# x goes to DRAM once in float32: the sum of its two parts, written by GpSimd over the half batch's own output tile

## The chip, the core and the metric

The kernel runs on one NeuronCore of a Trainium2 chip. The metric is device time in microseconds (us) of one execution; lower is better. Three runs of the kernel before took 1088.52, 1089.51 and 1095.21 us (median 1089.51).

## What is computed

Attention over 4 batches, 8 heads, 576 positions and head size 64, in which only scores within tau of the row's maximum count, and then two gated layers over the 2304 tokens, each 512 to 2048 to 512:

```python
scores = scale * q @ k.T                       # per batch and head
scores = where(scores >= max(scores) - tau, scores, -1e9)
x  = softmax(scores) @ v                       # 2304 x 512 after joining heads
h  = x @ w_in;   x1 = (h * clip(h + 3, 0, 6) / 6) @ w_out
h2 = x1 @ w2_in; out = (h2 - tanh(h2)) @ w2_out
```

All inputs and the output are float32. The kernel holds a float32 operand of a matmul as two parts, a high part and what is left (a low part), and multiplies them in three passes.

## The kernel before, in words

**The work in order of time.** Attention goes by 144 units (128 queries of one head, or the last 64 of two heads) in the order of half batches (b, g): 4 batches, 2 halves each. The scores of a unit are one group of matmuls (line 678); VectorE and ScalarE make the maximum, the exponential and the threshold (lines 683 to 694); ScalarE writes the high part of the weights and GpSimd the low part (`pp`, line 705); SyncE issues a DMA that transposes `pp` into `pt` (line 708); PE multiplies by the values (line 731), four units later; ScalarE takes the result into the output tile `x` of the half batch (line 738; `xl` for the last 64 queries).

When a half batch is complete, `x_round` turns its output into the operand of layer 1, in two or three pieces (i = 0, 1 and, in the second half, i = 2 for `xl`): reciprocal of the sums (lines 763, 766), normalising multiply on GpSimd (line 778; for the very last piece i = 1 on VectorE), four PE transposes (line 773), the high part by ScalarE (line 784) and the low part by VectorE (line 786) into `xT`, which has 128 partitions, two parts, 4 column blocks and up to 320 tokens. `layer1` (lines 819 to 863) then multiplies with the first half of the hidden units (8 groups of 128, weights kept in SBUF), gates, multiplies with the second matrix and stores a first part of the result to `ys`. It is interleaved with the attention of the next half batch; the last `layer1`, of half batch (3, 1), stands alone at about 488 to 525 us.

**Why x goes to DRAM.** The second half of the hidden units has no room beside the attention. Its weights (`bw`, `bo`) come into memory that the attention's tiles give back, and its nine blocks of 256 tokens read x again from DRAM. Before, `layer1` stores both parts of `xT` (two DMAs for each half batch, lines 828 and 829) into `xs`, and `load_x` loads both (two DMAs a block, line 1038), finds the largest value by a row sum (line 456), and makes scaled float16 parts: ScalarE the high part (line 1043), VectorE in two steps the low part (lines 1045 and 1048).

**What sets the order.** Every piece of work is recorded as a task with an engine, a modelled duration, a key (its priority) and its buffers, and `Plan.issue` (line 103) plays the tasks through a model once, when the program is built: an engine that is free takes the ready task with the lowest key. So each engine, and the DMA queue of SyncE, has a fixed order in the program. A task is ready when the writers of the tiles it reads, and all users of the buffer's previous content, are done. Dependencies are kept for a whole buffer, not for its parts. A new tile of the second stage can be made only after all users of the attention's rings (`at_rings`, to which `x` and `xl` belong but `xT` does not; line 970) are done: this is the task `second_memory` (line 972). On the chip a tile that lies on memory of the attention waits for the last user of that memory.

Then comes layer 2, from about 711 us to the end, with weights prepared through DRAM.

Of the kernel before, what the change touches and what calls it, by code (L numbers as in the profile page):

```python
# [9 lines left out]
F32 = mybir.dt.float32  # L10
# [5 lines left out]
ACTF = mybir.ActivationFunctionType  # L16
ALU = mybir.AluOpType
# [183 lines left out]
def attention_moe_moe_kernel(  # L201
# [59 lines left out]
    XL, FO = 1, 7  # L261
# [18 lines left out]
    xs = dram.tile([128, 2, KD, NT], F32, name="xs")  # L280
    ys = dram.tile([128, KD, NT], F32, name="ys")
    NB = 256
# [464 lines left out]
    def x_round(b, g, i, key):  # L747
# [29 lines left out]
        def norm():  # L777
# [5 lines left out]
        add("pe", 0.00085 * KD * w, key, tr, r=[xt], w=[tp, xT])  # L783
        hi = add("act", t_act(KD * w), key + RK, lambda: nc.scalar.activation(
            out=xT.t[:, 0, :, cols], in_=pv(), func=ACTF.Copy), r=[tp], w=[xT])
        add("dve", t_dve(KD * w), key + RK, lambda: nc.vector.tensor_tensor(
            out=xT.t[:, 1, :, cols], in0=pv(), in1=xT.t[:, 0, :, cols].bitcast(F32), op=ALU.subtract),
            r=[tp], w=[xT], after=[hi])

# [29 lines left out]
    def layer1(b, g, W, key, width):  # L819
# [7 lines left out]
        x_stores[b, g] = [  # L827
            add("dma", 0.47, key + width * (1 + part) / 4, lambda part=part: nc.sync.dma_start(
                out=xs[:, part, :, c0:c0 + n], in_=xT.t[:, part, :, 0:n].bitcast(F32)), r=[xT], xfer=1.6)
            for part in range(2)]  # L830
# [34 lines left out]
    with tc.manual_schedule():  # L865
# [136 lines left out]
        R_xf = ring2([128, 2, KD, NB], F32, "xf", slot1=2)  # L1002
# [30 lines left out]
        def load_x(i, c, n, key):  # L1033
            xf, x = R_xf.new(), R_xh.new()
            after = writers(c, n)
            part = lambda i: xf.t[:, i, :, 0:n]
            for h in range(2):
                add("dma", 0.47, key - 16.0 + h, lambda h=h: nc.sync.dma_start(
                    out=part(h), in_=xs[:, h, :, c:c + n]), w=[xf], after=after, xfer=1.6)
            a = row_sums(lambda: part(0), xmax[:, i:i + 1], lambda: x.t[:, 0, :, 0:n], [xf], [x], key - 10.0, KD * n)  # L1040
            a = common(xmax[:, i:i + 1], top_x[i % 2], xpow[:, 0, i:i + 1], xpow[:, 1, i:i + 1], 2.0 ** -6, key - 9.0, [a])
            s = xpow[:, 1, i:i + 1]
            hi = add("act", t_act(KD * n, sbuf=True, scalars=True), key - 6.0, lambda: nc.scalar.activation(
                out=x.t[:, 0, :, 0:n], in_=part(0), func=ACTF.Copy, scale=s), r=[xf], w=[x], after=[a])
            lo = add("dve", t_dve(KD * n, scalars=True), key - 5.0, lambda: nc.vector.scalar_tensor_tensor(
                out=part(0), in0=part(0), scalar=s, in1=x.t[:, 0, :, 0:n],
                op0=ALU.mult, op1=ALU.subtract), r=[x], w=[xf], after=[hi])
            add("dve", t_dve(KD * n, scalars=True), key - 4.5, lambda: nc.vector.scalar_tensor_tensor(  # L1048
                out=x.t[:, 1, :, 0:n], in0=part(1), scalar=s, in1=part(0),
                op0=ALU.mult, op1=ALU.add), r=[xf], w=[x], after=[lo])  # L1050
            u = lambda k: unscale[:, k, i:i + 1]
            b = add("dve", 0.15, key - 3.5, lambda: nc.vector.tensor_scalar(
                out=u(0), in0=xpow[:, 0, i:i + 1], scalar1=wmax["bi"][:, 1:2], scalar2=GS,
                op0=ALU.mult, op1=ALU.mult), after=[a, scaled["bi"]])
            b2 = add("dve", 0.15, key - 2.5, lambda: nc.vector.tensor_scalar(
                out=u(1), in0=u(0), scalar1=wmax["bo"][:, 1:2], scalar2=1.0 / (6.0 * GS * GS * GS2),
                op0=ALU.mult, op1=ALU.mult), after=[b, scaled["bo"]])
            x_ready[i] = [b], [b2]
            return x
# [537 lines left out]
```

## Time and profile before

| what | value |
|---|---|
| median of three runs | 1089.51 us |
| the profiled execution | 1088.51 us, of which its span is 1086.7 us |
| PE busy | 1015.0 us (93%) |
| VectorE (DVE) busy | 847.6 us (78%) |
| ScalarE (ACT) busy | 718.6 us (66%) |
| GpSimd (POOL) busy | 339.0 us (31%), nearly all of it before 525 us |
| TensorE's granted clock, mean of the execution | 0.964 of full speed |

Busy time is summed over the instructions of an engine. A busy PE is not PE at its peak, since matmuls are pipelined and their ends are modelled. The stages differ, so the shares must be read by stretches of time.

### The profile page before, as it was taken

Reading aid. Unit: us, or ns where it says so; the run is one execution under the profiler, and the core shown is the slowest. Engines: PE = TensorE matmul, PEld = TensorE weight load, DVE = VectorE, ACT = ScalarE, POOL = GpSimd, SP = SyncE. Lnnn points to the kernel's source line nnn. Section 1 sums busy time; section 2 is a strip of 40 time slices with the busy share of each in tenths; the row PEclk is TensorE's granted clock in tenths of the full one; section 3 lists DMA queues with packets and bytes.
Section 4 is the critical chain, followed back from the end, with each engine's and each line's share of the span. In section 5 each row is a group of like instructions: output and inputs, shape, how many; then the busy total and the mean of one; then the engine's idle time right before and its main releaser. Section 6 shows DMA issues by size and latency. Waiting matters only on the chain.

```text
span 1086.7 us, 23294 instructions
## 1 busy us (share of the span) xinstructions
PE 1015.0 (93%) x8984; PEld 838.6 (77%) x8984; DVE 847.6 (78%) x1630; ACT 718.6 (66%) x1312; POOL 339.0 (31%) x353
## 2 busy tenths in 40 slices
PE   5668799999999899988999999999999999999998
PEld 4557788998999799978988888876676666666664
DVE  5889977687869788758797778889976796784564
ACT  6867979687967786645675566756755675574332
POOL 2656757666855675623000000000001111121000
PEclk8668899999999989998999999999999999999999
DMA  7899688967899989978657755432333866573335
GB/s 184 165 222 213 132 159 182 196 132 158 187 181 192 205 175 216 219 159 261 201 173 257 253 199 185 165 108 97 107 117 118 208 131 117 126 127 51 87 92 142
DMA packets 285007, 179.27 MB, mean 165 GB/s; under 512 B 202976, under 2 KB 257760, under 8 KB 284896
## 3 DMA queue, kind: packets, MB, share of 16 engines
q1 hardware_dynamic: 279088, 168.07, 61.0%
q0 software_dynamic: 5184, 9.44, 6.5%
q8 instruction: 71, 1.16, 0.5%
q14 instruction: 40, 0.33, 0.1%
q10 hardware_dynamic: 624, 0.26, 0.1%
HBM read 89.13 MB, written 46.14 MB: 124 GB/s over the span
## 4 chain that ended last, share of the span: by engine, by line
PE 58%; DVE 4%; ACT 1%; DMA 1%; issue 0%; SPq 0%; ACTq 0%; DVEq 0%
PE ya L489 24%; PE m L489 16%; PE h L489 10%; PE m L850 3%; PE s L678 2%; PE tp L731 1%; DMA y<-y 1%; PE h L850 1%; PE m L476 0%; DVE x L1276 0%; DMA st<-in_moe_w_in_dram 0%; DVE xh L1048 0%; DVE t L803 0%; PE tp L561 0%; DVE y L1175 0%
## 5 line engine op out<-in xcount | busy, mean ns | idle before, releaser
L705 POOL TENSOR_TENSOR pp<-e,pp 128x128 f16<-128x128 f32 (+3 forms) x156 | 181.1, 1182 | 120.3 <-issue 54.1
L489 PE MATMUL ya<-wo,g 128*128 128x512 f16 x864 | 205.4, 379 | 1.0 <-DVE g L813 0.6
L489 PEld LDWEIGHTS <-wi 128*128 128x128 f16 x1536 | 150.0, 98 | 40.4
L1416 POOL DMA_DIRECT2D po<-o x36 | 31.2, 876 | 459.7 <-ACT o L1410 459.7
L489 PEld LDWEIGHTS <-g 128*128 128x128 f16 x864 | 84.1, 98 | 79.3 <-DVE g L813 1.1
L683 DVE TENSOR_REDUCE z<-s 128x1 f32<-128x576 f32 x144 | 107.9, 753 | 45.4 <-PE s L678 44.7
L694 DVE SCALAR_TENSOR_TENSOR e<-s,z,e 128x576 f32<-128x576 f32 x144 | 115.8, 811 | 22.1 <-ACT e L685 17.1
L678 PE MATMUL s<-ks,q 128*128 128x288 f32 x512 | 105.9, 337 | 20.9 <-DVE e L694 20.1
L685 ACT ACTIVATE e<-s,z 128x576 f32<-128x576 f32 x144 | 105.0, 739 | 26.6 <-DVE z L683 20.3
L489 PE MATMUL m<-xT,ai 128*128 128x256 f32 (+1 forms) x720 | 112.8, 301 | 1.8 <-DVE st L426 0.6
L678 PEld LDWEIGHTS s<-ks,q 128*128 128x128 f32 x512 | 82.4, 212 | 29.4 <-DVE e L694 13.4
L489 PEld LDWEIGHTS m<-xT,ai 128*128 128x128 f32 x720 | 99.3, 190 | 3.7 <-DVE st L426 1.1
L489 PE MATMUL ya<-g,bo 128*128 128x256 f16 x864 | 101.1, 273 | 0.5 <-DVE g L813 0.5
L731 PE MATMUL tp<-vt,pt 128*128 128x65 f16 (+1 forms) x2240 | 88.4, 199 | 8.5 <-ACT q L591 2.4
L489 PE MATMUL m<-x,wi 128*128 128x256 f16 x768 | 95.2, 273 | 0.0
L731 PEld LDWEIGHTS <-pt 128*128 128x128 f16 (+1 forms) x2240 | 79.8, 104 | 16.7 <-DMA pt<-pp 6.0
L1381 ACT ACTIVATE t<-t,hid_s 128x512 f32<-128x512 f32 x72 | 51.6, 718 | 62.0 <-DVE t L1372 61.4
L489 PEld LDWEIGHTS <-bo 128*128 128x128 f16 x864 | 84.1, 98 | 10.6 <-issue 0.9
L489 PEld LDWEIGHTS <-bw 128*128 128x128 f16 x864 | 84.1, 98 | 10.4 <-issue 0.4
L813 DVE SCALAR_TENSOR_TENSOR g<-g,t 128x512 f16<-128x512 f16 x108 | 73.8, 686 | 20.7 <-ACT g L809 20.2
L809 ACT ACTIVATE g<-t 128x512 f16<-128x512 f32 x108 | 67.0, 624 | 33.7 <-DVE t L1383 26.0
L699 ACT ACTIVATE pp<-e 128x1152 f16<-128x1152 f32 (+1 forms) x80 | 85.1, 1064 | 5.0 <-DVE e L694 4.7
(177 smaller groups left out, 1878.0 us busy)
## 6 DMA issues: line engine op xcount, KB each, us to landing
st<-in_moe_w_in_dram SPq DMA_DIRECT2D x40, 512.0 KB, 5.0
st<-in_moe_w_out_dram SPq DMA_DIRECT2D x40, 512.0 KB, 4.4
xf<-xs SPq DMA_DIRECT2D x18, 512.0 KB, 5.2
y<-y SPq DMA_DIRECT2D x18, 512.0 KB, 3.8
po<-o POOLq DMA_DIRECT2D x36, 256.0 KB, 4.2
xs<-xT SPq DMA_DIRECT2D x8, 640.0 KB, 4.9
y<-ys SPq DMA_DIRECT2D x9, 512.0 KB, 5.9
po<-o SPq DMA_DIRECT2D x18, 256.0 KB, 2.0
```

The costliest lines, as they stand in the source:

```text
L489: nc.tensor.matmul(ps, l[a], r[b], start=first and t == 0 and i == 0, stop=last and t == 2 and i == n - 1,)
L678: nc.tensor.matmul(ps.t[:, half, 0:SH], l, ks[:, half * SH:(half + 1) * SH], start=i == 0, stop=i == len(ops) - 1,)
L683: add("dve", 0.69, key, lambda: nc.vector.tensor_reduce(out=z.t[:, 0:1], in_=s(), axis=AX.XY, op=ALU.max, negate=True), r=[ps], w=[z])
L685: exp = add("act", 0.66, key, lambda: nc.scalar.activation(out=ex(), in_=s(), func=ACTF.Exp, bias=z.t[:, 0:1]), r=[ps, z], w=[e])
L694: add("dve", 0.74, key, lambda: nc.vector.scalar_tensor_tensor(out=ex(), in0=s(), scalar=z.t[:, 1:2], in1=ex(), op0=ALU.is_ge, op1=ALU.mul ...
L699: high = add("act", t_act(w * S, sbuf=True), key, lambda: nc.scalar.activation(out=pp.t[:, 0:w, 0:S], in_=e.t[:, 0:w, :], func=ACTF.Copy), ...
L705: add(eng, dur, key, lambda src=src, dst=dst, queue=queue: queue.tensor_tensor(out=pp.t[:, 0:w, dst], in0=e.t[:, 0:w, src], in1=pp.t[:, 0: ...
L731: nc.tensor.matmul(pv.t[0:m, w_ * (D + 1):(w_ + 1) * (D + 1)], pt.t[:, n, blk, rows], vv, start=o == 0, stop=o == len(ops) - 1)
L809: hi = add("act", t_act(n, sbuf=True), key, lambda: nc.scalar.activation(out=gh(), in_=t(), func=ACTF.Copy, scale=GS2 if far else 1.0), r= ...
L813: go = lambda: nc.vector.scalar_tensor_tensor(out=gl(), in0=gh(), scalar=1.0 / GS2, in1=t(), op0=ALU.mult, op1=ALU.subtract)
L850: prev = [add("pe", t_mm(n, 1), kd, lambda p=p, l=l, r=r, m=m, s=s, ps=ps: nc.tensor.matmul(ps.t[:, 0:n], W["o", m].t[:, l, s], r[m].t[:, ...
L1381: add("act", t_act(2 * NB, sbuf=True, scalars=True), key, lambda: nc.scalar.activation(out=s_(), in_=h.t, func=ACTF.Tanh, scale=c), r=[h], ...
```

## The change

`xs` has room for one float32 array instead of two parts. After the high and the low part of a piece are in `xT`, GpSimd adds them (the transposed, normalised x) and writes the sum over the half batch's own output tile `x` (or `xl`), whose content has been transposed by then; a DMA stores it from there. Each piece is its own addition and its own DMA: 16 pieces of 128 tokens (512 elements a partition, runs of 512 bytes in DRAM) and 4 of 64 tokens (256 elements, runs of 256 bytes). The two stores of `layer1` fall away. `load_x` loads one array, and one VectorE step makes the low part.

```diff
-    xs = dram.tile([128, 2, KD, NT], F32, name="xs")
+    xs = dram.tile([128, KD, NT], F32, name="xs")
...
+    XL, FO, XWK = 1, 7, 12.0
...
-        add("pe", 0.00085 * KD * w, key, tr, r=[xt], w=[tp, xT])
+        turned = add("pe", 0.00085 * KD * w, key, tr, r=[xt], w=[tp, xT])
...
+        c0 = b * S + g * 256 + i * 128
+        xw = lambda: xt.t[:, c].rearrange("p h d -> p (h d)")[:, 0:KD * w].rearrange("p (k n) -> p k n", k=KD)
+        add("pool", t_pool(KD * w), key + XWK, lambda: nc.gpsimd.tensor_tensor(
+            out=xw(), in0=xT.t[:, 0, :, cols].bitcast(F32), in1=xT.t[:, 1, :, cols].bitcast(F32), op=ALU.add),
+            r=[xT], w=[xt], after=[lo, turned])
+        x_stores.setdefault((b, g), []).append(add("dma", 0.47, key + XWK + 2.0, lambda: nc.sync.dma_start(
+            out=xs[:, :, c0:c0 + w], in_=xw()), r=[xt], xfer=0.00625 * w))
...
-        x_stores[b, g] = [
-            add("dma", 0.47, key + width * (1 + part) / 4, lambda part=part: nc.sync.dma_start(
-                out=xs[:, part, :, c0:c0 + n], in_=xT.t[:, part, :, 0:n].bitcast(F32)), r=[xT], xfer=1.6)
-            for part in range(2)]
...
-        R_xf = ring2([128, 2, KD, NB], F32, "xf", slot1=2)
+        R_xf = ring2([128, KD, NB], F32, "xf", slot1=2)
...
-            for h in range(2):
-                add("dma", 0.47, key - 16.0 + h, lambda h=h: nc.sync.dma_start(
-                    out=part(h), in_=xs[:, h, :, c:c + n]), w=[xf], after=after, xfer=1.6)
+            add("dma", 0.47, key - 16.0, lambda: nc.sync.dma_start(
+                out=raw(), in_=xs[:, :, c:c + n]), w=[xf], after=after, xfer=1.6)
...
-            lo = add("dve", t_dve(KD * n, scalars=True), key - 5.0, lambda: nc.vector.scalar_tensor_tensor(
-                out=part(0), in0=part(0), scalar=s, in1=x.t[:, 0, :, 0:n],
-                op0=ALU.mult, op1=ALU.subtract), r=[x], w=[xf], after=[hi])
-            add("dve", t_dve(KD * n, scalars=True), key - 4.5, lambda: nc.vector.scalar_tensor_tensor(
-                out=x.t[:, 1, :, 0:n], in0=part(1), scalar=s, in1=part(0),
-                op0=ALU.mult, op1=ALU.add), r=[xf], w=[x], after=[lo])
+            add("dve", t_dve(KD * n, scalars=True), key - 5.0, lambda: nc.vector.scalar_tensor_tensor(
+                out=x.t[:, 1, :, 0:n], in0=raw(), scalar=s, in1=x.t[:, 0, :, 0:n],
+                op0=ALU.mult, op1=ALU.subtract), r=[xf], w=[x], after=[hi])
```

In the changed kernel the lines from 784 on stand a few lines lower or higher; the new addition is line 791, the new store line 794, the new load line 1040, and old lines 803, 1126 and 1128 are 810, 1125 and 1127.

**GpSimd, at the end of the first half batch** (`x` the output tile, `ao` and `ai` weights of layer 1, `pp` the attention weights). Before:

```order
L705 TENSOR_TENSOR pp<-e,pp 128x512
L778 TENSOR_TENSOR x<-x,rx 128x512
L451 TENSOR_TENSOR ao_1125<-st,ao_1125 128x512
L778 TENSOR_TENSOR x<-x,rx 128x512
L554 COPY qr<-qr 128x4x64
L705 TENSOR_TENSOR pp<-e,pp 128x2x64
L705 TENSOR_TENSOR pp<-e,pp 128x2x512
```

With the change:

```order
L705 TENSOR_TENSOR pp<-e,pp 128x512
L778 TENSOR_TENSOR x<-x,rx 128x512
L451 TENSOR_TENSOR ao_1125<-st,ao_1125 128x512
L554 COPY qr<-qr 128x4x64
L791 TENSOR_TENSOR x<-xT 128x512
L705 TENSOR_TENSOR pp<-e,pp 128x2x64
L451 TENSOR_TENSOR ai_1202<-st,ai_1202 128x512
L778 TENSOR_TENSOR x<-x,rx 128x512
```

The addition of the first piece stands ahead of a `pp`, and the normalising of the second piece has moved behind that addition, because both write the one buffer `x`.

**VectorE, at the end of the last half batch, about 482 to 490 us** (`rx`, `rl` reciprocals, `wu` and `st` weights of the second half, `tp` the bank of the transposes). Before:

```order
L763 SCALAR_TENSOR_TENSOR rx_7962<-x_7078,sv_5718 128x16
L766 RECIPROCAL rx_7962<-rx_7962 128x16
L778 TENSOR_TENSOR x_7078<-x_7078,rx_7962 128x512
L763 SCALAR_TENSOR_TENSOR rl_8006<-xl_7244,sv_5718 64x8
L766 RECIPROCAL rl_8006<-rl_8006 64x8
L786 TENSOR_TENSOR xT_8014<-tp_8000,xT_8014 128x4x128
L786 TENSOR_TENSOR xT_8014<-tp_8009,xT_8014 128x4x128
L418 TENSOR_SCALAR wu_8019<-wu_8019 128x512
L420 TENSOR_SCALAR wu_8019<-wu_8019 128x512
L786 TENSOR_TENSOR xT_8014<-tp_8022,xT_8014 128x4x64
```

With the change:

```order
L763 SCALAR_TENSOR_TENSOR rl_8020<-xl_7247,sv_5724 64x8
L766 RECIPROCAL rl_8020<-rl_8020 64x8
L786 TENSOR_TENSOR xT_8029<-tp_8023,xT_8029 128x4x128
L418 TENSOR_SCALAR wu_8038<-wu_8038 128x512
L778 TENSOR_TENSOR x_7083<-x_7083,rx_7980 128x512
L786 TENSOR_TENSOR xT_8029<-tp_8032,xT_8029 128x4x64
L420 TENSOR_SCALAR wu_8038<-wu_8038 128x512
L418 TENSOR_SCALAR wu_8044<-wu_8044 128x512
L423 SCALAR_TENSOR_TENSOR wu_8038<-st_7978,wu_8038 128x512
L786 TENSOR_TENSOR xT_8029<-tp_8047,xT_8029 128x4x128
```

The normalising of the second piece (line 778) has moved from ahead of the first low part (line 786) to behind it, and behind one step on weights; the second piece's low part, now the last of the three, stands behind three such steps.

**SyncE's DMA queue and ScalarE, at the change of memory, about 482 to 500 us** (`xs` in DRAM, `xf` the loaded x, a wait on DMAHW*n* is for an earlier DMA of that number). SyncE before:

```order
L406 DMA st_7960<-in_moe_w_in_dram 128x4x256 [waits DMAHW7_49]
L406 DMA st_7965<-in_moe_w_in_dram 128x4x256
L406 DMA st_7968<-in_moe_w_in_dram 128x4x256 [waits DMAHW1_49]
L828 DMA xs_60<-xT_8014 128x4x320 [waits Activation_49]
L1038 DMA xf_8055<-xs_60 128x4x256 [waits DMAHW3_49,DMAHW5_49,PE_49,Pool_49]
L1038 DMA xf_8055<-xs_60 128x4x256 [waits DMAHW4_49]
L1038 DMA xf_8068<-xs_60 128x4x256
L1038 DMA xf_8068<-xs_60 128x4x256 [waits DMAHW6_49]
L828 DMA xs_60<-xT_8014 128x4x320 [waits DMAHW7_49,DVE_49]
L406 DMA st_8102<-in_moe_w_in_dram 128x4x256 [waits DMAHW0_49,DVE_49]
```

With the change:

```order
L406 DMA st_7978<-in_moe_w_in_dram 128x4x256
L406 DMA st_7983<-in_moe_w_in_dram 128x4x256 [waits DMAHW3_49]
L406 DMA st_8017<-in_moe_w_in_dram 128x4x256
L794 DMA xs_60<-x_7083 512x1x128 [waits DMAHW5_49,Pool_49]
L794 DMA xs_60<-x_7083 512x1x128 [waits DMAHW6_49,Pool_49]
L794 DMA xs_60<-xl_7247 512x1x64 [waits DMAHW7_49,Pool_49]
L1040 DMA xf_8143<-xs_60 128x4x256 [waits DMAHW5_49,DMAHW6_49,DMAHW0_49,DMAHW7_49,PE_49,Activation_49]
L1040 DMA xf_8146<-xs_60 128x4x256 [waits DMAHW1_49]
L406 DMA st_8171<-in_moe_w_in_dram 128x4x256 [waits DMAHW2_49,DVE_49]
```

ScalarE with the change, over the same stretch:

```order
L807 ACTIVATE t_8082<-m_8058,three_131 128x320 [waits DMAHW7_49,PE_49,Activation_49]
L807 ACTIVATE t_8095<-m_8076,three_131 128x320 [waits DMAHW0_49,PE_49,Activation_49]
L816 ACTIVATE gh0_8103<-t_8082 128x320 [waits DVE_49]
L816 ACTIVATE gh2_8113<-t_8095 128x320 [waits DVE_49]
L1125 ACTIVATE bw_8141<-st_7978,wmax_122 128x512 [waits DMAHW6_49,DMAHW5_49,DMAHW7_49,Activation_49,Pool_49]
L1125 ACTIVATE bw_8152<-st_7983,wmax_122 128x512 [waits DVE_49]
L807 ACTIVATE t_8164<-m_8136,three_131 128x320 [waits DMAHW1_49,PE_49]
```

The three stores of the last half batch take the numbers 5, 6 and 7. With the change both the first load of `xf` and the first `bw` wait for these three; before, the stores read `xT` and neither waited for them.

## Rows read from the trace of the kernel before

**Rows 1.** The page's part 1: busy us, share of the span, instructions of each engine.

```profile
PE 1015.0 (93%) x8984; PEld 838.6 (77%) x8984; DVE 847.6 (78%) x1630; ACT 718.6 (66%) x1312; POOL 339.0 (31%) x353
```

**Rows 2.** Stretches of time: length, busy us of each engine, PEclk, DMA share, GB/s.

```profile
85.00:478.00 393.00, 368.67 (x4109) 348.04 (x4109) 309.89 (x588) 301.48 (x585) 249.60 (x252) 0.97 0.87 179
478.00:525.00 47.00, 39.62 (x308) 37.10 (x307) 36.00 (x83) 24.97 (x48) 12.66 (x10) 0.93 0.82 245
525.00:1071.00 546.00, 542.63 (x4134) 404.18 (x4133) 428.26 (x834) 327.79 (x559) 31.25 (x36) 1.00 0.52 145
```

**Rows 3.** Waits of PE, 85 to 478 us: total us, times, longest.

```profile
PE s L678 <- DVE e L694: 14.4, 14, 4.9
PE tp L731 <- DMA pt<-pp: 0.3, 1, 0.3
```

**Rows 4.** Groups on GpSimd by form: busy us, mean ns, idle before.

```profile
L816 POOL TENSOR_TENSOR gl<-t,gh 128x256 fp32r<-128x256 f32 x32 | 23.5, 738 | 15.7 <-ACT gh L809 15.3
L778 POOL TENSOR_TENSOR x<-x,rx 128x512 f32<-128x512 f32 x15 | 15.9, 1074 | 13.4 <-DVE rx L766 13.4
L451 POOL TENSOR_TENSOR ao<-st,ao 128x512 fp32r<-128x512 f32 x8 | 10.5, 1308 | 5.3 <-ACT ao L448 5.3
```

**Rows 5.** Instructions on the tile xf: min/median/max ns, first and last start us.

```profile
L1045 DVE SCALAR_TENSOR_TENSOR xf<-xf,xpow,xh x9: 1275/1278/1286, 503.5 to 678.1; 128x1024 f32<-128x1024 f32 x9
L1048 DVE SCALAR_TENSOR_TENSOR xh<-xf,xpow x9: 1268/1276/1767, 505.6 to 682.4; 128x1024 f16<-128x1024 f32 x9
```

**Rows 6.** Timeline, 482 to 491 us: start us, us, instruction, idle before and releaser.

```profile
483.21 0.69 DVE L778 TENSOR_TENSOR x<-x,rx 128x512 f32<-128x512 f32 x1
483.32 1.48 POOL L778 TENSOR_TENSOR x<-x,rx 128x512 f32<-128x512 f32 x1 [11.08 <-DVE rx L766]
...
484.86 1.09 PE L773 MATMUL tp<-ident,x 128*128 128x128 f32 x8
...
485.55 1.09 ACT L784 ACTIVATE xT<-tp 128x512 fp32r<-128x512 f32 x2 [0.40 <-PE tp L773]
...
486.80 0.69 ACT L414 ACTIVATE wu<-st 128x512 f32<-128x512 f32 x1 [0.16 <-DMA st<-in_moe_w_in_dram]
...
487.52 0.43 DVE L418 TENSOR_SCALAR wu<-wu 128x512 f32<-128x512 f32 x1
...
487.92 3.00 PE L489 MATMUL m<-xT,ai 128*128 128x320 f32 x12 [0.47 <-ACT xT L784]
...
488.32 0.42 DVE L786 TENSOR_TENSOR xT<-tp,xT 128x256 fp32r<-128x256 f32 x1
488.42 3.04 SPq L1038 DMA_DIRECT2D xf<-xs  x4
...
488.65 0.68 DVE L423 SCALAR_TENSOR_TENSOR wu<-st,wu 128x512 int32<-128x512 int32 x1
...
490.36 0.78 ACT L1126 ACTIVATE bw<-st,wmax 128x512 f16<-128x512 f32 x1 [1.26 <-DVE st L426]
```

**Rows 7.** The same view, 495 to 513 us.

```profile
495.78 1.05 ACT L456 ACTIVATE xh<-xf 128x1024 f16<-128x1024 f32 x1
...
511.83 0.47 ACT L809 ACTIVATE gh<-t 128x320 fp32r<-128x320 f32 x1 [3.94 <-DVE t L803]
...
511.85 0.85 PE L850 MATMUL h<-gh,ao 128*128 128x320 f32 x4 [2.82 <-DVE t L803]
```

**Rows 8.** A stretch after PE's idle at 480 to 488 us, columns as Rows 2.

```profile
490.00:492.00 2.00, 2.00 (x9) 2.00 (x8) 1.97 (x5) 1.64 (x3) 0.00 (x0) 0.50 0.92 186
```

**Rows 9.** DMA issues: instructions, KB each, median us from issue to landing.

```profile
xf<-xs SPq DMA_DIRECT2D x18, 512.0 KB, 5.2
xs<-xT SPq DMA_DIRECT2D x8, 640.0 KB, 4.9
wdo<-wu SPq DMA_DIRECT2D x16, 256.0 KB, 2.7
left<-in_k_dram SPq DMA_DIRECT2D x4, 128.0 KB, 4.7
```

More of the change, by code (lines that the diff above doesn't have):

```diff
@@ L260, in attention_moe_moe_kernel @@
     LK, LQ, LV, LD = 5, 3, 1, 4
-    XL, FO = 1, 7
+    XL, FO, XWK = 1, 7, 12.0
     XL3 = 40.0
@@ L782, in x_round @@
         add(*(("dve", t_dve(DM)) if tail else ("pool", t_pool(DM))), key - 7.0, norm, r=[xt, rx], w=[xt])
-        add("pe", 0.00085 * KD * w, key, tr, r=[xt], w=[tp, xT])
+        turned = add("pe", 0.00085 * KD * w, key, tr, r=[xt], w=[tp, xT])
         hi = add("act", t_act(KD * w), key + RK, lambda: nc.scalar.activation(
             out=xT.t[:, 0, :, cols], in_=pv(), func=ACTF.Copy), r=[tp], w=[xT])
-        add("dve", t_dve(KD * w), key + RK, lambda: nc.vector.tensor_tensor(
+        lo = add("dve", t_dve(KD * w), key + RK, lambda: nc.vector.tensor_tensor(
             out=xT.t[:, 1, :, cols], in0=pv(), in1=xT.t[:, 0, :, cols].bitcast(F32), op=ALU.subtract),
             r=[tp], w=[xT], after=[hi])
+        c0 = b * S + g * 256 + i * 128
[5 more added lines that the diff above has]
+            out=xs[:, :, c0:c0 + w], in_=xw()), r=[xt], xfer=0.00625 * w))
     def t_half(n, count):
@@ L1035, in load_x @@
             after = writers(c, n)
-            part = lambda i: xf.t[:, i, :, 0:n]
-            for h in range(2):
-                add("dma", 0.47, key - 16.0 + h, lambda h=h: nc.sync.dma_start(
-                    out=part(h), in_=xs[:, h, :, c:c + n]), w=[xf], after=after, xfer=1.6)
-            a = row_sums(lambda: part(0), xmax[:, i:i + 1], lambda: x.t[:, 0, :, 0:n], [xf], [x], key - 10.0, KD * n)
+            raw = lambda: xf.t[:, :, 0:n]
+            add("dma", 0.47, key - 16.0, lambda: nc.sync.dma_start(
+                out=raw(), in_=xs[:, :, c:c + n]), w=[xf], after=after, xfer=1.6)
+            a = row_sums(raw, xmax[:, i:i + 1], lambda: x.t[:, 0, :, 0:n], [xf], [x], key - 10.0, KD * n)
             a = common(xmax[:, i:i + 1], top_x[i % 2], xpow[:, 0, i:i + 1], xpow[:, 1, i:i + 1], 2.0 ** -6, key - 9.0, [a])
@@ L1043, in load_x @@
             hi = add("act", t_act(KD * n, sbuf=True, scalars=True), key - 6.0, lambda: nc.scalar.activation(
-                out=x.t[:, 0, :, 0:n], in_=part(0), func=ACTF.Copy, scale=s), r=[xf], w=[x], after=[a])
-            lo = add("dve", t_dve(KD * n, scalars=True), key - 5.0, lambda: nc.vector.scalar_tensor_tensor(
-                out=part(0), in0=part(0), scalar=s, in1=x.t[:, 0, :, 0:n],
-                op0=ALU.mult, op1=ALU.subtract), r=[x], w=[xf], after=[hi])
-            add("dve", t_dve(KD * n, scalars=True), key - 4.5, lambda: nc.vector.scalar_tensor_tensor(
-                out=x.t[:, 1, :, 0:n], in0=part(1), scalar=s, in1=part(0),
-                op0=ALU.mult, op1=ALU.add), r=[xf], w=[x], after=[lo])
+                out=x.t[:, 0, :, 0:n], in_=raw(), func=ACTF.Copy, scale=s), r=[xf], w=[x], after=[a])
+            add("dve", t_dve(KD * n, scalars=True), key - 5.0, lambda: nc.vector.scalar_tensor_tensor(
+                out=x.t[:, 1, :, 0:n], in0=raw(), scalar=s, in1=x.t[:, 0, :, 0:n],
+                op0=ALU.mult, op1=ALU.subtract), r=[xf], w=[x], after=[hi])
             u = lambda k: unscale[:, k, i:i + 1]
```

## Prediction

> **What bounds the kernel now.** I read the shares of the span first: PE is busy 93% of it, VectorE 78%, GpSimd 31% [rows 1]. These are means over unlike stages, so the table by stretches came next [rows 2]. From 525 to 1071 us PE is busy 542.6 of 546.0 us: whatever another engine saves there is hidden, up to 3.4 us. In the attention, 85 to 478 us, PE is busy 368.7 of 393.0 us and leaves 24.3 us; GpSimd is busy 249.6 us (64%). The waits show what PE stood still for: 14.4 us for VectorE's thresholded scores, but only 0.3 us for the transposed weights that come from GpSimd by way of a DMA [rows 3]. So GpSimd has slack there. In 478 to 525 us, where the attention ends and its memory changes hands, PE leaves 7.4 us. The timeline of that stretch is the one to read closely [rows 6, 7], since the change touches it in two places.
>
> **The change, part by part.**
>
> *Layer 1's second half, 525 us on.* Nine VectorE steps fall away, each with a median of 1.28 us [rows 5], together 11.5 us, and nine of eighteen loads of 512 KB [rows 9]. PE covers all of this [rows 2]: I take nothing, with a gain of at most 3.4 us. Were the cover gone, the 11.5 us would count.
>
> *Attention: the additions.* Before the last half batch there are 14 additions of 512 elements and 3 of 256. The trace has no such addition; nearest are GpSimd's normalising multiply of the same size, 1.07 us, and its subtraction of two float32 tiles of that size, 1.31 us; for 256 elements 0.74 us [rows 4]. With 1.19 between the two, 14 x 1.19 + 3 x 0.74 = 18.9 us. GpSimd goes from 249.6 to about 268 us of 393 (68%). I take nothing on the path, because PE hardly waits for what GpSimd makes [rows 3]; the cover is GpSimd's idle and the four units that the weighting lags behind. Without the cover it is all 18.9 us. Below nothing the bound is the 14.4 us that PE waits for VectorE: another order could shorten them, and nothing excludes it.
>
> *Attention: the second piece behind the first.* The planner holds dependencies for the whole buffer, so the second piece's normalising now waits until the first piece has been turned, split and added. PE's work at these places is otherwise the scores of the next half batch, which are ready; I take nothing, except at the end, where no next half batch follows.
>
> *The stores.* Two of up to 640 KB for each half batch become two or three of 256 or 128 KB, 20 for 16, with half the bytes. The DMA engines are busy 87% of the attention [rows 2], but PE does not wait for them; nothing.
>
> *The end of the attention.* Here the price is. First, the last piece's normalising on VectorE stood at 483.21 us [rows 6]. Now it stands behind the step of line 418, which ended at 487.95 because ScalarE's step before it had waited for a weight DMA until 486.80 [rows 6]. Then come 0.69 for the normalising, half of 1.09 for its four transposes, half of 1.09 for the high part [rows 6]: 489.7 instead of the 487.92 at which PE began, so 1.8 us late. Its low part now stands behind the other piece's (0.42) and three weight steps (0.43, about 0.43 and 0.68): from 488.64 to 490.6, and 0.69 more gives 491.3. Before, the last low part ended at 488.74. Second, the tiles of the next stage wait for the three stores, as the order shows. The addition of the piece (1.19) and of the short one (0.74) end at 493.2; for a store the nearest row is a 256 KB store from SBUF, 2.7 us to landing [rows 9], which makes 495.9. ScalarE's first `bw`, before at 490.36, comes 5.5 us later. The loads of x go out at 495.9 instead of 488.42, and with 5.2 us to landing [rows 9] the row sum of line 456 starts at 501.1 instead of 495.78: 5.3 us late. Between it and the last gate (511.83 us) VectorE did four steps of 1.28 us; two remain, which gives 2.6 back [rows 5]. The gate, and with it PE's second product at 511.85 [rows 7], come 5.3 - 2.6 = 2.7 us late, and nothing behind it is idle enough to win them back [rows 2].
>
> A bound above for the last store: it writes runs of 256 bytes, and the only rows with such runs, 128 KB loads of k, take 4.7 us [rows 9], 2.0 us more. The Trainium skill speaks against this piece: "DMA: Bandwidth & Descriptors", Specifications, asks for at least 512 bytes a transfer for full rate and says that below this the engine reads, modifies and writes. By that rule the term would be 4.7 us instead of 2.7; no store with such runs is in the trace, so it does not decide. I stay with the store row, since half the bytes go. If ScalarE, not VectorE, carries the gate, the 2.6 us don't come back: 5.3. PE also ran at half clock (0.50, 1.2 GHz) in 490 to 492 us after its idle [rows 8]; a longer idle can add about 1 us of that. Ends: 2.7 + 2.0 + 2.6 + 1.0 = 8.3 us above; below, the stretch's whole idle gone, -7.4 us.
>
> *Sum.* The rows are of an execution of 1088.51 us (span 1086.7 and 1.8 around it). 0 + 0 + 2.7 gives 1091.2. The median of the runs is 1.0 above that execution, so 1092.2 us on the scale of the median.
>
> **The rivals.**
>
> *The transition costs nothing.* PE has eight groups of matmuls of the last layer 1 in front of it, and six can run before a bank must come back; ScalarE's 3.94 us and PE's 2.82 us of idle before the gate [rows 7] may swallow the delay. Then the median stays at 1089.5. Against it: those idles are VectorE's backlog, and the loads now start 7 us later. Chance 0.20.
>
> *Faster.* VectorE's backlog bounds 478 to 525 us (it is busy 36.0 of 47.0 [rows 2]), and it loses two of four large steps there, while the DMAs move half the bytes. If the stores land early enough that only this counts, the idle of the stretch goes: 1089.5 - 7.4 = 1082.1, and with the 3.4 us behind it 1078.7. It decides if the row sum starts before about 498 us. Chance 0.13.
>
> *Slower: GpSimd's queue.* GpSimd runs in order. An addition waits for VectorE's low part, and the weights' low part (`pp`) behind it waits too, then the transposing DMA, then PE. Of the 17 additions before the last half batch, 10 stand right ahead of a `pp`, two of them short: 8 x 1.19 + 2 x 0.74 = 11.0 us, so 1103; with all 17 it is 18.9, so 1111. It decides once the delay is longer than the lag of four units covers. For it: GpSimd is idle in pieces, not as a block. Against it: the 0.3 us [rows 3]. Chance 0.18.
>
> *Slower: both engines at one port.* GpSimd's multiply that ran beside VectorE's at 483.2 took 1.48 us [rows 6], where the mean is 1.07 [rows 4]: 0.41 longer. If each of 20 additions loses or costs that once on the path, 8.2 us: about 1100. Against it: most of VectorE's work in the attention takes one input from PSUM. Chance 0.07. The Trainium skill ("SBUF — State Buffer", Who interferes with whom) has the rule: a GpSimd instruction that reads SBUF and a VectorE instruction with two SBUF inputs share a port, and the later one is blocked entirely. The longer row agrees in kind, at 0.41 us.
>
> **How the numbers follow.** The forecast has 0.42, the rivals 0.20, 0.13, 0.18 and 0.07. The time is the forecast's, 1092.2; its own range is about 1088 to 1098. The range from 1082 to 1106 takes in the stretch's idle gone on one side, and additions that stand ahead of a `pp` on the other; what is left out is the far half of the faster case and of GpSimd's queue. One per cent, about what a measurement of this kernel can tell from no change, is 10.9 us: below 1078.6 or above 1100.4. Faster: the faster case's far end and some luck in the attention's order, 0.08. Slower: three quarters of GpSimd's queue, half of the port and the forecast's upper tail, 0.18. The same: 0.74.
>
> **What would show it.** Right: the first `bw` and the row sum near 496 and 501 us with a DMA as what they waited for; PE's gap before its second product still there and some 2.7 us later; from there to the end the same length as before; 85 to 478 us within 3 us. Wrong: PE waiting for `pt` by several us in the attention (GpSimd's queue); `pp` or VectorE steps longer where an addition runs (the port); the row sum at or before 498 us, or a span of 525 to 1071 us that shrinks by more than 3.4 us, which would say that PE's busy time there hides a wait.

## The result, and the profile after

The kernel before has a median of 1089.28 us over 15 runs, the changed one 1097.14 us (1092.32 to 1100.37, 15 runs): a ratio of 1.0062, 95% interval [1.0047, 1.0077]. That is slower by 0.6%, inside the one per cent that I called the same, and 4.9 us above the forecast of 1092.2. The profiled execution of the changed kernel took 1094.55 us (span 1092.8), 6.1 us longer in span than the one of before, and is itself 2.6 us below the median of its runs.

The page's part 1 of the changed kernel answers to [rows 1]:

```profile
PE 1016.1 (93%) x8984; PEld 841.0 (77%) x8984; DVE 839.5 (77%) x1621; ACT 718.8 (66%) x1312; POOL 362.6 (33%) x373
```

GpSimd has 20 instructions and 23.6 us more, VectorE nine instructions and 8.1 us less. The three stretches of [rows 2] again (length, busy us of each engine in the order PE, weight load, VectorE, ScalarE, GpSimd, then the granted clock, DMA share, GB/s):

```profile
85.00:478.00 393.00, 365.37 (x4082) 345.74 (x4081) 307.17 (x587) 300.74 (x583) 268.70 (x269) 0.97 0.83 169
478.00:525.00 47.00, 38.44 (x295) 35.84 (x295) 34.43 (x76) 22.88 (x45) 16.62 (x13) 0.89 0.57 162
525.00:1071.00 546.00, 543.63 (x4143) 406.73 (x4143) 423.60 (x830) 330.50 (x563) 31.32 (x36) 1.00 0.51 142
```

PE is as full as before from 525 us on. The waits of PE between 85 and 478 us, for [rows 3]:

```profile
PE s L678 <- DVE e L694: 15.9, 14, 2.6
...
PE tp L731 <- DMA pt<-pp: 0.7, 2, 0.4
```

So GpSimd's 19 us more still do not reach PE by way of the transposed weights. Most of the time went into the end of the attention, as a_last_dma below shows. Here is its timeline in the changed kernel (start us, us, instruction, idle before and what ended it), to be read beside [rows 6]:

```profile
485.25 1.04 POOL L778 TENSOR_TENSOR x<-x,rx 128x512 f32<-128x512 f32 x1 [12.77 <-DVE wmax L1112]
...
488.50 1.26 POOL L791 TENSOR_TENSOR x<-xT 128x512 f32<-128x512 f32 x1 [0.73 <-DVE xT L786]
...
488.86 1.20 DVE L418 TENSOR_SCALAR wu<-wu 128x512 f32<-128x512 f32 x1 [0.49 <-ACT wu L414]
...
489.97 0.68 DVE L778 TENSOR_TENSOR x<-x,rx 128x512 f32<-128x512 f32 x1
...
490.80 0.63 PE L773 MATMUL tp<-ident,x 128*128 128x128 f32 x4 [2.51 <-DVE x L778]
...
492.11 6.89 PE L489 MATMUL m<-xT,ai 128*128 128x320 f32 x36 [0.69 <-ACT xT L784]
...
492.94 1.66 POOL L791 TENSOR_TENSOR x<-xT 128x512 f32<-128x512 f32 x1 [3.17 <-DVE xT L786]
493.38 1.51 DVE L420 TENSOR_SCALAR wu<-wu 128x512 int32<-128x512 int32 x1
...
494.57 0.92 POOL L791 TENSOR_TENSOR xl<-xT 128x256 f32<-128x256 f32 x1
494.81 0.96 DVE L418 TENSOR_SCALAR wu<-wu 128x512 f32<-128x512 f32 x1
495.51 0.51 SPq L794 DMA_DIRECT2D xs<-xl  x1
...
497.80 1.54 SPq L1040 DMA_DIRECT2D xf<-xs  x2
...
498.79 1.39 ACT L1125 ACTIVATE bw<-st,wmax 128x512 f16<-128x512 f32 x2
```

The new order can be followed line by line: the first piece's multiply (485.25), its addition (488.50), only then the second piece's multiply on VectorE (489.97), PE's first product of layer 1 at 492.11 instead of 487.92, the last addition, the last store (495.51), and when it has landed the loads of x (497.80 instead of 488.42) and the first `bw` (498.79 instead of 490.36). The waits of SyncE's queue show that the loads did stand for that store (us, times, longest):

```profile
SPq L1040 <- DMA xs<-xl: 0.6, 1, 0.6
```

The timeline further on, for [rows 7], with the gate's product (516.22 us, 511.85 before) and the first product of the second half of the hidden units (530.11 us, 524.48 before):

```profile
502.76 1.04 ACT L456 ACTIVATE xh<-xf 128x1024 f16<-128x1024 f32 x1
...
516.22 1.44 PE L853 MATMUL h<-gh,ao 128*128 128x320 f32 x4 [2.59 <-DVE t L810]
...
530.11 2.79 PE L489 MATMUL m<-xh,bw 128*128 128x256 f16 x24
```

From there to the end it is 562.7 us, before 1086.7 - 524.48 = 562.2. The DMA issues that answer to [rows 9] (KB each, median us to landing):

```profile
xf<-xs SPq DMA_DIRECT2D x9, 512.0 KB, 4.4
xs<-x SPq DMA_DIRECT2D x16, 256.0 KB, 3.0
...
xs<-xl SPq DMA_DIRECT2D x4, 128.0 KB, 2.3
```

### The profile page after: what moved, and what is told of

Read it like the earlier page. It is cut to its first block, busy times and chain, and to the rows that moved or that the text cites. A ratio compares the mean times of both kernels' runs of the same rounds, so it can differ in the third digit from the quotient of the medians.

```text
span 1092.8 us, 23307 instructions
## 1 busy us (share of the span) xinstructions
PE 1016.1 (93%) x8984; PEld 841.0 (77%) x8984; DVE 839.5 (77%) x1621; ACT 718.8 (66%) x1312; POOL 362.6 (33%) x373
## 4 chain that ended last, share of the span: by engine, by line
PE 83%; DVE 7%; ACT 4%; DMA 3%; issue 2%; SPq 1%; POOL 0%; DVEq 0%; ACTq 0%; POOLq 0%
PE ya L489 25%; PE m L489 22%; PE h L489 11%; PE m L853 8%; PE s L678 7%; PE tp L731 6%; DVE e L694 2%; PE tp L561 2%; DMA pt<-pp 1%; DVE z L683 1%; DVE ks L586 1%; ACT ks L584 1%; PE h L853 1%; ACT e L685 1%; PE m L476 1%
## 5 line engine op out<-in xcount | busy, mean ns | idle before, releaser
L694 DVE SCALAR_TENSOR_TENSOR e<-s,z,e 128x576 f32<-128x576 f32 x144 | 116.2, 812 | 12.6 <-ACT e L685 6.4
L678 PEld LDWEIGHTS s<-ks,q 128*128 128x128 f32 x512 | 83.4, 215 | 36.1 <-DVE e L694 22.7
L489 PEld LDWEIGHTS m<-xT,ai 128*128 128x128 f32 x720 | 102.2, 195 | 3.6 <-DVE t L810 1.5
```

The source lines that it names most:

```text
L489: nc.tensor.matmul(ps, l[a], r[b], start=first and t == 0 and i == 0, stop=last and t == 2 and i == n - 1,)
L678: nc.tensor.matmul(ps.t[:, half, 0:SH], l, ks[:, half * SH:(half + 1) * SH], start=i == 0, stop=i == len(ops) - 1,)
L694: add("dve", 0.74, key, lambda: nc.vector.scalar_tensor_tensor(out=ex(), in0=s(), scalar=z.t[:, 1:2], in1=ex(), op0=ALU.is_ge, op1=ALU.mul ...
```

## A mark to count from

All executions come to the end of the attention at different times, so I count from one event: the start of GpSimd's last multiply of line 778 on `x`, called the mark. It lies at 483.32 us before and at 485.25 in the changed kernel. In the changed kernel and in the experiments below that edit its last half batch alone, the instructions stand in the same order up to there; the kernel before has another order. Four columns are us behind the mark, from the timelines, the fourth of them the end of the span. PE idle and PE busy are what lies between the mark and the first product `xh,bw`; the last column is the ratio to the kernel before.

| kernel | mark | first `bw` | row sum, line 456 | first product `xh,bw` | end | PE idle | PE busy | ratio, 95% |
|---|---|---|---|---|---|---|---|---|
| before | 483.32 | 7.0 | 12.5 | 41.2 | 603.4 | 5.2 | 35.9 | 1 |
| changed | 485.25 | 13.5 | 17.5 | 44.9 | 607.6 | 8.0 | 36.9 | 1.0062 [1.0047, 1.0077] |
| after_again | 488.91 | 14.3 | 18.3 | 44.4 | 606.0 | 7.3 | 37.1 | 1.0046 [1.0028, 1.0064] |
| a_last_dma | 483.66 | 6.8 | 11.2 | 39.1 | 601.1 | 5.2 | 33.9 | 0.9986 [0.9968, 1.0004] |
| b_last_order | 487.01 | 10.6 | 14.8 | 43.1 | 606.1 | 6.6 | 36.6 | 1.0047 [1.0029, 1.0066] |
| b_last_again | 489.81 | 10.7 | 14.8 | 43.3 | 605.7 | 6.6 | 36.7 | 1.0042 [1.0026, 1.0059] |
| f_serial | 489.12 | 11.4 | 16.0 | 42.8 | 604.6 | 6.7 | 36.1 | 1.0018 [1.0003, 1.0032] |
| f_serial_again | 489.93 | 11.4 | 15.9 | 40.1 | 602.1 | 6.0 | 34.1 | 1.0014 [0.9998, 1.0030] |
| h_adds_only | 485.99 | 8.8 | 11.9 | 42.9 | 604.8 | 6.7 | 36.2 | 1.0041 [1.0022, 1.0059] |

Between the first product `xh,bw` and the end every one of them needs 561.6 to 563.0 us. So the price stands ahead of that product: in the 41 us behind the mark, and in when the mark comes.

Even behind the mark one execution is not like another of the same program. f_serial and f_serial_again differ by 2.7 us at the first product, 2.0 of it in PE's busy time, for the same matmuls. The stretch from 24 to 28 us behind the mark shows what differs (columns as [rows 2]; f_serial first):

```profile
513.12:517.12 4.00, 4.00 (x18) 3.98 (x18) 3.24 (x8) 3.34 (x7) 2.89 (x2) 0.57 0.21 51
513.93:517.93 4.00, 3.49 (x24) 3.22 (x22) 3.70 (x7) 2.83 (x5) 2.37 (x3) 1.00 0.80 249
```

The granted clock was 0.57 in one, mostly the half level of 1.2 GHz, and full (2.4 GHz) in the other. So two microseconds of busy time between two lines of the table can be the clock's and need not be the edit's.

## The experiments

**The whole end of the attention undone: a_last_dma.** Theory: the price is made in the last half batch. Rival: GpSimd's queue in the attention. The last half batch has no addition; the transposed tile is stored as before, with the low part accumulated onto the high one by a DMA.

```diff
+        if (b, g) != (B - 1, 1):
             add("pool", ...)  # the addition and its store
...
+        if (b, g) == (B - 1, 1):
+            x_stores[b, g] = [add("dma", ..., lambda: nc.sync.dma_start(
+                out=xs[:, :, c0:c0 + n], in_=xT.t[:, 0, :, 0:n].bitcast(F32)), ...)]
+            x_stores[b, g].append(add("pool", ..., lambda: nc.gpsimd.dma_start(
+                out=xs[:, :, c0:c0 + n], in_=xT.t[:, 1, :, 0:n].bitcast(F32), accum_op=ALU.add), ...))
```

> The changed kernel, but the last half batch alone sends x to DRAM from the operand tile xT, its high part by a store and its low part by an accumulating DMA from GpSimd; there is no addition and no store from the output tile at the end of the attention. Theory 1 (the price is made at the end of the attention, by the second piece that waits for the first and by the next stage's tiles that wait for three late stores): the first bw goes back from 498.8 to about 491 us, the row sum from 502.8 to about 497 us, PE's second product comes 4 to 6 us earlier, and the time falls from 1097.1 to about 1092 us. Theory 2 (GpSimd's additions delay the attention before that): at most 1 us comes back, about 1096 us. Theory 3 (VectorE is the bound at the gate, whatever the loads do): the row sum comes earlier but the second product stays near 516 us, about 1096 us.

Measured: 1088.97 us, ratio 0.9986 [0.9968, 1.0004]. The timeline of the end of the attention:

```profile
487.85 2.03 PE L489 MATMUL m<-xT,ai 128*128 128x320 f32 x12 [0.50 <-ACT xT L784]
...
488.54 1.89 SPq L1047 DMA_DIRECT2D xf<-xs  x2
...
490.45 0.76 ACT L1132 ACTIVATE bw<-st,wmax 128x512 f16<-128x512 f32 x1
...
494.82 1.06 ACT L456 ACTIVATE xh<-xf 128x1024 f16<-128x1024 f32 x1 [0.84 <-DMA xf<-xs]
```

Product, loads and `bw` stand where they stood in [rows 6], although the other 17 additions still run. Undoing the last half batch alone takes the whole price away, and the time is 3 us below the 1092 that I expected. The run undoes additions, order and stores together.

**The order of its pieces undone: b_last_order, b_last_again.** The second piece's multiply no longer stands behind the first one's addition. The additions, the stores and the wait for them stay.

```diff
+        end = (b, g) == (B - 1, 1)
...
-            r=[xT], w=[xt], after=[lo, turned])
+            r=[xT, xt] if end else [xT], w=[] if end else [xt], after=[lo, turned])
...   # the store now names the addition as what it waits for
```

> The changed kernel, with one dependency less in the planner for the last half batch: the second piece's normalising no longer waits for the first piece's addition, while the three stores from the output tile stay, and with them the wait of the next stage's tiles. Theory 1: the first product of the last layer 1 starts about 2.5 us earlier (489.6 instead of 492.1 us), the stores land about 2 us earlier, and the time falls by 1.5 to 2.5 us to about 1095 us; the difference to the kernel without the stores is what the wait for memory costs, about 3 us. If the order of the pieces is the whole price, it falls by 5 to about 1092 us; if it is none of it, it stays at 1097.

> b_last_order once more: if the order is worth as much beside the stores as it was without them (f_serial against a_last_dma, 3.9 us), 4 us below the change of this call; if the wait for the stores hides most of it, 1 to 2 us below.

Measured: 1096.14 us (1.0047) and 1094.99 us (1.0042), the latter 1.3 us below the changed kernel that ran beside it (after_again). Of the first, the products and what the next stage waits for:

```profile
491.22 6.51 PE L489 MATMUL m<-xT,ai 128*128 128x320 f32 x32 [0.52 <-ACT xT L784]
...
496.15 1.25 SPq L1041 DMA_DIRECT2D xf<-xs  x2
...
497.62 0.74 ACT L1126 ACTIVATE bw<-st,wmax 128x512 f16<-128x512 f32 x1
```

The first product is back to 4.2 us behind the mark (6.9 in the changed kernel), yet nearly all of the price is left: beside the stores, the order is worth 1 us or so by the medians, which these runs can't tell from nothing.

**The additions elsewhere: d_double_add.** Every addition of the first seven half batches runs twice.

```diff
-        add("pool", ..., lambda: nc.gpsimd.tensor_tensor(...)
+        add("pool", ..., lambda: [nc.gpsimd.tensor_tensor(...)
+            for _ in range(1 if (b, g) == (B - 1, 1) else 2)],
```

> The changed kernel in the same order, with every addition of the first seven half batches done twice on GpSimd (17 more instructions, about 20 us of GpSimd time). Theory 1 (the additions in the attention are hidden): no more than 1.5 us, about 1098 us, and PE's waits for the transposed weights stay under 2 us in 85 to 478 us. Theory 2 (GpSimd's queue carries the additions to the path): 10 to 19 us more, 1107 to 1116 us, PE waiting for pt or VectorE's scores later by that. A port shared with VectorE: VectorE's steps of the attention get longer where an addition runs, 3 to 8 us more, about 1102 us.

Measured: 1098.43 us, 1.0068 [1.0050, 1.0086]; the changed kernel's interval holds it. Stretch and wait, 85 to 478 us (two views):

```profile
85.00:478.00 393.00, 366.65 (x4046) 346.68 (x4044) 304.88 (x584) 300.67 (x582) 287.91 (x285) 0.95 0.81 167
```

```profile
PE tp L731 <- DMA pt<-pp: 0.6, 2, 0.4
```

GpSimd does 19.2 us more, PE waits as little for the transposed weights, and the median is 1.3 us above the changed kernel's, 2.2 above after_again's, where this rival wanted 10 or more. The rival of GpSimd's queue falls.

**The saving alone: e_high_only.** No addition; the high part alone goes to DRAM from the transposed tile and is loaded. The low part of x is left out of the second half of the hidden units. So half the stores, half the loads and the nine VectorE steps are saved, and nothing is paid.

```diff
-        add("pool", ...)  # the addition and its store, for all half batches
...
+        x_stores[b, g] = [add("dma", ..., lambda: nc.sync.dma_start(
+            out=xs[:, :, c0:c0 + n], in_=xT.t[:, 0, :, 0:n].bitcast(F32)), ...)]
```

> The changed kernel without any addition: the high part of x alone is stored from xT, one store for each half batch, and loaded again (the low part of x is left out of the second half of the hidden units). It has what the change saves, half the stores, half the loads and one VectorE step for each block, and none of what it adds. Theory 1: the saving is worth little, since PE covers it from 525 us on, but VectorE's backlog before the gate at 511.8 us shrinks by two steps: 1089.3 - 2.5 = about 1087 us. If the saving is wholly hidden: 1089. If the DMA engines bounded the attention: under 1083.

Measured: 1090.06 us, 0.9995 [0.9978, 1.0012]. My 1087 was a miss: the saving is worth nothing that can be measured. PE still stands at the same gate:

```profile
512.21 1.11 PE L850 MATMUL h<-gh,ao 128*128 128x320 f32 x5 [2.80 <-DVE t L805]
```

It is 28.5 us behind the mark before, 29.4 here (mark 482.86). The row sum starts at 495.99, so from it to the gate it is 16.2 us as before (16.1), with two large VectorE steps fewer between.

**Order and additions kept, no store from the output tile: f_serial, f_serial_again.** Only what is sent to DRAM differs: x goes from the transposed tile as in a_last_dma. The next stage still has to wait for the three additions over the output tile, but for no store from it.

```diff
+        if (b, g) != (B - 1, 1):
             x_stores.setdefault((b, g), []).append(...)   # the store from the output tile
...
+        if (b, g) == (B - 1, 1):
+            ...   # the store and the accumulating DMA of a_last_dma
```

> The last half batch keeps its three additions over the output tile and the order in which its second piece stands behind the first one's addition; but nothing is stored from the output tile, and x goes to DRAM from the transposed tile as in the run a_last_dma. If the order of the pieces makes the price: PE's first product at about 492 us as in the change, the row sum at 500 us or later, and a ratio to the kernel before of 1.004 to 1.006 (1094 to 1096 us). If the wait for the three late stores makes it: first product still near 492 us, but the loads of x go out 3 us or more earlier than in the change, and the ratio is 0.998 to 1.002. If both share it: the row sum near 499 us and a ratio near 1.003.

> f_serial once more: a ratio of 1.000 to 1.003, and if the wait for the stores is the larger half of the price, 4 us or more below the change of this call.

Measured: 1092.87 us (1.0018) and 1092.31 us (1.0014); the latter stands 3.9 us below the changed kernel that ran beside it. The first:

```profile
496.44 5.38 PE L489 MATMUL m<-xT,ai 128*128 128x320 f32 x24 [0.69 <-ACT xT L784]
...
499.76 1.44 SPq L1047 DMA_DIRECT2D xf<-xs  x2
...
500.52 0.75 ACT L1132 ACTIVATE bw<-st,wmax 128x512 f16<-128x512 f32 x1
```

The product is as late as in the changed kernel (7.3 us behind the mark), the `bw` 2.1 us nearer to it. So with this order kept, going without these stores gave back 3.9 of the 5.8 us by which the changed kernel that ran beside it lay above the kernel before. My signs were met only in part: the ratio is that of "the wait for the stores", but the loads of x came 1.9 us nearer to the mark (10.6 us behind it, 12.55 in the changed kernel) where I wanted 3, and 3.9 is just short of the 4 that I asked for in the second run.

**Neither, but the additions: h_adds_only.** b_last_order's edit and f_serial's together.

```diff
+        end = (b, g) == (B - 1, 1)
...
-            r=[xT], w=[xt], after=[lo, turned])
+            r=[xT, xt] if end else [xT], w=[] if end else [xt], after=[lo, turned])
+        if (b, g) != (B - 1, 1):
             x_stores.setdefault((b, g), []).append(...)   # the store from the output tile
...
+        if (b, g) == (B - 1, 1):
+            ...   # the store and the accumulating DMA of a_last_dma
```

> The fourth case of two: the last half batch keeps its three additions, but its second piece does not stand behind the first one's (as in b_last_order), and nothing is stored from the output tile (as in f_serial). If only the order and the wait for the stores cost: as a_last_dma, a ratio to the kernel before of 0.997 to 1.000 (1087 to 1090 us), first product near 488 us. If the additions themselves cost, because the next stage's tiles wait for GpSimd's last one: 1.001 to 1.003 (1091 to 1093 us), the first bw 2 us or more after that of a_last_dma.

Measured: 1095.14 us, 1.0041 [1.0022, 1.0059]: over the 1093 that I had for the additions, and no better than with the stores. Its timeline, with a wait of SyncE's queue behind it, shows what three additions do:

```profile
489.25 2.69 POOL L792 TENSOR_TENSOR x<-xT 128x512 f32<-128x512 f32 x2 [0.45 <-DVE xT L786]
...
491.06 1.17 DVE L420 TENSOR_SCALAR wu<-wu 128x512 int32<-128x512 int32 x1
...
491.90 0.93 POOL L792 TENSOR_TENSOR xl<-xT 128x256 f32<-128x256 f32 x1
492.15 0.97 DVE L418 TENSOR_SCALAR wu<-wu 128x512 f32<-128x512 f32 x1
...
492.86 2.18 SPq L1048 DMA_DIRECT2D xf<-xs  x2
```

```profile
SPq L1048 <- POOL xl L792: 2.1, 1, 2.1
```

The loads wait for the last addition, 2.0 us later behind the mark than in a_last_dma, and VectorE's weight steps stretch. In a_last_dma, without additions, the same steps take 0.42 us:

```profile
487.62 0.42 DVE L418 TENSOR_SCALAR wu<-wu 128x512 f32<-128x512 f32 x1
487.95 0.42 DVE L786 TENSOR_TENSOR xT<-tp,xT 128x256 fp32r<-128x256 f32 x1
488.28 0.42 DVE L420 TENSOR_SCALAR wu<-wu 128x512 int32<-128x512 int32 x1
```

So the price is not a sum of an order and a wait. Without the stores, keeping the serial order (f_serial_again) measured 2.8 us lower than undoing it (h_adds_only, run beside it); the planner places all that follows anew in each, and which of those moves does it stays open. The traces don't settle it: PE's idle time behind the mark is 6.7 us in h_adds_only, 6.7 and 6.0 in the two of f_serial, 5.2 in a_last_dma, so by these traces the additions alone leave 0.8 to 1.5 us of idle in either order, and the rest of the differences at the first product is busy time, in which the clock has a part.

**The order elsewhere, and two candidates.** b_all_order takes the dependency of b_last_order away in all half batches; ab_order_dma does that in the first seven and a_last_dma's edit in the last; c_accum has no addition at all, and every half batch lets a DMA accumulate the low part.

```diff
-            r=[xT], w=[xt], after=[lo, turned])
+            r=[xT, xt], w=[], after=[lo, turned])   # b_all_order; ab_order_dma also has a_last_dma's lines
```

```diff
-        add("pool", ...)  # c_accum: no addition, no store of xt
+        x_stores[b, g] = [...]   # a_last_dma's two DMAs, for every half batch
```

> For every half batch, not the last alone, the second piece no longer stands behind the first one's addition; the additions and the stores from the output tile stay. If the order of the pieces costs nothing in 85 to 478 us, as I predicted: the same as the run b_last_order, a ratio of 1.004 to 1.006 (about 1096 us). If it costs something there: 2 us or more below that run, 1094 us or less.

> The edit of b_all_order for the first seven half batches, and for the last one the stores of a_last_dma (high part, then the low part accumulated onto it by a DMA, both from the transposed tile). If the order costs nothing in 85 to 478 us: as a_last_dma, a ratio of 0.997 to 1.000 (1087.5 to 1090 us). If the order costs there: 0.996 or less, faster than both kernels.

> No addition on GpSimd at all: every half batch stores its high part and lets a GpSimd DMA accumulate the low part onto it in DRAM, from the transposed tile; behind it x is loaded once in float32 as in the change. If the additions are wholly hidden: as a_last_dma, a ratio of 0.997 to 1.000. If they cost what doubling them cost (1 to 2 us): 0.996 to 0.998. If the accumulating DMAs, which read and write DRAM, disturb the weight transposes (PE waiting over 3 us for the transposed weights in 85 to 478 us): 1.002 or more.

Measured: 1098.21 us (1.0068 [1.0043, 1.0094]), 1093.16 us (1.0030 [1.0011, 1.0049]) and 1099.65 us (1.0081 [1.0061, 1.0101]). Freeing the order in the attention gains nothing. It measured 2 us above b_last_order, within the noise, and 4 us above a_last_dma, where the intervals do not overlap and I had expected no cost; why is not traced. c_accum's end is good (594.8 us from its first product of layer 1 to the end of the span, 598.8 before), but that product comes at 503.94 us. Part of that is a wait that [rows 3] did not have:

```profile
PE tp L731 <- DMA pt<-pp: 3.6, 2, 3.4
```

Seven of its eight accumulating DMAs, 1.2 us each to issue, stand in GpSimd's queue there. The rest of its 16 us is not traced. No version beats the kernel before by more than its measurement is uncertain. The changed kernel itself, run once more:

> The change itself once more, beside the other cases: a ratio of 1.005 to 1.008 (1095 to 1098 us).

It measured 1096.25 us, 1.0046 [1.0028, 1.0064]: the ratio a little under what I expected, the time inside it.

## Why the prediction was right, and where its size was off

**525 us on: nothing.** Right. PE is busy 543.6 of 546.0 us; e_high_only, with the saving and no price, ends level with the kernel before.

**The additions in the attention: hidden.** Right: GpSimd is busy 268.7 us there (268 forecast), PE waits 0.7 us for its weights, and doubling the additions changes next to nothing.

**The second piece behind the first, elsewhere; the stores: nothing.** Not quite right. One wait of PE of over 3 us is new in the attention, at the end of the first half batch, where the order of GpSimd put the second piece's multiply behind the first one's addition and PE's four transposes of that piece came late too. Before, then in the changed kernel:

```profile
92.21 1.09 PE L773 MATMUL tp<-ident,x 128*128 128x128 f32 x4
```

```profile
100.59 1.08 PE L773 MATMUL tp<-ident,x 128*128 128x128 f32 x4 [3.22 <-DVE q L593]
```

By the trace, what ended the wait was VectorE's step on `q`; the multiply itself was done by 95.6 us. The wait is 3.4 us in after_again and 4.3 with the additions doubled, and b_all_order, which undoes the order, does not have it. Over 85 to 478 us, at the same granted clock (0.97), PE is idle 27.6 us instead of 24.3, and the mark comes at 485.25 instead of 483.32. But its price in the whole time is not shown: the mark of one program lies anywhere in 6 us, and b_all_order and ab_order_dma, without the wait, did not measure lower.

**The end of the attention.** Counted from the mark, the chain came as forecast. The loads of x were forecast at 495.9 - 483.32 = 12.6 us, and came at 12.55; the row sum at 17.8, and came at 17.5; the gate at 31.2, and came at 516.22 - 485.25 = 31.0. Inside this sum two terms were off and partly cancelled: the two additions took 2.6 us (492.94 to 495.49) where I had 1.9, and the last store landed in 2.2 where I had 2.7. The bound for that store was not needed. The four stores of 128 KB in runs of 256 bytes landed in 2.3 us (median), those of 256 KB in 3.0. The Trainium skill's rule that I weighed there ("DMA: Bandwidth & Descriptors", Specifications) would have made it the slow one; the landing of one such store shows no sign of it, and no run here measures a rate.

**The term that was mis-sized is the sum at this place: 2.7 us forecast, 6.1 us between the two spans.** 1.9 of it is the mark itself. 2.4 is the gate (28.5 us behind the mark before, 31.0 after), as forecast; in after_again it is 3.3. The other 1.7 come behind the gate: 1.3 from it to the first product `xh,bw`, and 0.5 from there on. That 1.3 is the clock. From the gate to that product (before, changed, after_again):

```profile
511.85:524.48 12.63, 12.63 (x75) 12.53 (x75) 9.24 (x15) 5.63 (x10) 1.10 (x1) 0.86 0.70 218
516.22:530.11 13.89, 13.89 (x75) 13.79 (x76) 9.34 (x17) 4.92 (x9) 3.02 (x1) 0.78 0.58 180
520.78:533.27 12.49, 12.49 (x75) 12.38 (x76) 9.33 (x17) 4.95 (x9) 3.02 (x1) 0.88 0.69 197
```

PE is busy throughout with the same 75 recorded matmuls, and the longer stretch is the one with the lower granted clock; length times clock is 10.8 to 11.0 us in all three. The prediction had this only at the upper end of its range (1.0 us for half clock after a longer idle), not in the sum, and after_again does not show it. By the ratio the whole is 6.8 us, and 5.0 when run again. So behind the mark the forecast's 2.7 fits what two profiles show, 4.2 and 2.6 us to the end of the span; what lies ahead of the mark was put at nothing, and how much of the 5 to 7 us stands there stays open.

**The 2.6 us given back.** From the row sum to the gate it is 13.5 us instead of 16.1, just what I forecast. But e_high_only lost the same two VectorE steps and has 16.2. So fewer steps are not shown to be the reason; that the gate had other work ahead of it, which let 2.6 us of a late row sum go by, fits both. The number was right, its reason is not proved.

**The port.** I gave it 0.07 and counted 0.41 us for each addition. In the last half batch it is more. The three weight steps that met an addition took 1.20, 1.51 and 0.96 us instead of 0.42: 2.4 us of VectorE's time just where VectorE is the engine waited for, and the first of them holds back the second piece's multiply by 0.8. They end 0.30, 0.29 and 0.28 us after the addition's end. The Trainium skill ("SBUF — State Buffer", Who interferes with whom) says that the two engines take their shared port in turn, whole instructions at a time; these ends agree, for VectorE steps with one input tile. The forecast's sum left this out. What it cost is not shown: the gate came when the sum without it said.

**The transition costs nothing.** It fell: the gate came 2.4 to 3.3 us later and the ratio's interval excludes 1, though PE's idle ahead of the gate did shrink, from 2.82 us to 2.59 and 1.74.

**Faster.** It needed the row sum before 498 us; it came at 502.76. The half loads, by e_high_only, would have brought nothing even then.

## What to carry to other kernels

Price a new reader of a buffer by who gets the memory next: an addition and a store for each half batch cost 5 to 7 us in the whole, and nothing once the eighth went without them; there the tiles of the next stage had waited for them. Before paying for a saving, measure the saving alone: here half of the loads and nine VectorE steps were worth nothing. When executions drift by microseconds, compare them from an event up to which both kernels are written alike, and set PE's idle time apart from its busy time, in which the clock hides.

## What the runs showed of the hardware

The mark, with the same instructions in the same order ahead of it, lay between 483.66 and 489.93 us in eight profiled executions, with a granted clock over 85 to 478 us between 0.98 and 0.95. So single spans of this kernel can't be compared to better than some 6 us.

After its wait PE began the products of layer 1 at half clock (1.2 GHz) in the changed kernel too, for about 3 us, and was back at 2.4 GHz from 496 us:

```profile
492.00:494.00 2.00, 1.89 (x7) 1.89 (x8) 2.00 (x4) 0.57 (x2) 1.06 (x1) 0.50 0.00 0
494.00:496.00 2.00, 2.00 (x12) 2.00 (x11) 1.77 (x2) 0.60 (x2) 1.49 (x2) 0.72 0.09 27
496.00:499.00 3.00, 3.00 (x23) 3.00 (x22) 2.21 (x5) 1.58 (x5) 0.71 (x1) 1.00 0.46 119
```

GpSimd's addition of two float32 tiles of 128x512 took 1.28 us (median of 16) and 1.66 where a step of VectorE was already running (492.94), where I had 1.19.
